# Local and pooled attention with a mixture of experts on one core: the first steps in another order, and the first slot's chain divided over the last two units

## The chip, the cores and the metric

The kernel runs on one core of a Trainium2 chip. The metric is the time of one launch on the device in microseconds. TensorE (PE in the rows) does the matrix products and transposes, VectorE (DVE) reductions and elementwise work, ScalarE (ACT) activations and copies, GpSimd (POOL) elementwise work and indirect transfers, and SyncE (SP) issues the plain transfers. The engines run beside one another; each takes its own instructions in the order of the program.

## The reference

The first half is two attentions over q, k and v of 8 batches, 8 heads, 576 positions and 64 features. One sees only the positions closer than 4; the other works on means over groups of 4 positions, and its result is repeated 4 times. Their sum, with the heads side by side, is x, 4608 rows of 512. The second half sends each row to one of 8 experts and weights the answer:

```python
mask = np.abs(pos[:, None] - pos[None, :]) < factor
attn_out = out_up + out_local
logits = xn @ en.T / tau              # xn, en: rows over their norms
expert_idx = np.argmax(logits, axis=1)
h = np.maximum(x[mask] @ w1[e], 0.0)
out[mask] = gate_w[mask, None] * (h @ w2[e])
```

## The kernel before

**Attention.** A unit is one batch and one pair of heads; there are 32, numbered 0 to 31. The function attention (lines 182 to 331 of the file before) is a loop over i from -2 to 32, and each step i holds one stage of three or four units: the transposes of q and k for unit i+2 (qk_T, L378, whose four results ACT copies out of PSUM at L379), the scores of unit i+1 (scores L407 and L412, scores_d L434 for the pooled half), and the weights and values of unit i (weights_T L485, weights_dT L496, values_d L505, values L521); rows (L536, L539) brings unit i-1 back to rows and forms logits. ACT and DVE do the softmax between them: the copies aT (L488) and adT (L498), the exponentials (L425, L454), the sums, their inverses, and the products an (L472) and ad (L477). od (L511) is the pooled result and xr (L543) the rows. The order of the Python statements is the order of each engine's queue; nothing else reorders it.

**Banks.** Every product goes to one of 7 PSUM banks of one pool (bank), handed out in rotation: a product that takes the bank of seven allocations ago waits until that one has been read. In a usual step the third bank of weights_T is that of the first of qk_T's four, so PE waits there for ACT's first copy of L379.

**Guests in the steps.** Between the steps the loop yields its place (i, k), and other generators run. first_weights (L904 to L970) brings expert 0's w1 and w2 in, in four pieces each: it loads a piece, squares it on ACT (L859) for a scale, adds up over partitions with one product (total, L868), works the power of two out on DVE (scales, L876 and L878, which ends in the tile wscl), and splits each piece into two f16 halves: the high one on ACT (split_h, L882), the low one on DVE one step later (split_l, L887). The three tuples FREE, LIGHT and HEAVY name the steps, modulo 4, in which the next piece may come. early_slots (L711 to L744) takes its turns at the places listed in EARLY. A slot is a block of 128 rows of one expert; the first three are filled from batches 0 to 5 while the attention still runs: limits, indices (ids_of, L702), a gather of rows on POOL (L1126), and then for slot 0 the chain x_size (a sum of squares on ACT, L1144, and a power of two on DVE, L79 to L81) and x_split (x's high half on ACT, L1153, its low half on DVE, L1156, and a transposing transfer, L1158). The first product of the experts (mm1_half, L1205 to L1207) needs that transfer.

**The start.** load brings q and k of 4 heads (two units), load_v and load_w bring v in two layouts. Constants are made on POOL and DVE meanwhile. warm_up (L337) is a number of products of 128x512 zeros whose results nobody reads.

Of the kernel before, what the change touches and what calls it, by code (L numbers as in the profile page):

```python
# [43 lines left out]
FIRST = 3  # L44
EARLY = ((28, 0), (28, 1), (29, 0), (30, 3), (31, 0), (31, 1))
MASKED = -1.0e30
# [5 lines left out]
class Kern:  # L52
# [55 lines left out]
    def constants_rows(self):  # L108
# [14 lines left out]
        nc.vector.memset(self.enT, 0.0)  # L123
        yield
# [56 lines left out]
    def attention(self, ctx):  # L181
# [28 lines left out]
        def load_w(j):  # L210
            if j < n // 2:
                self.load_w(j // 2, j % 2, self.vw[j % 2])

        load(0)
        nc.vector.memset(self.w1h[:, 0, :512], 0.0)
# [17 lines left out]
        next(crows)  # L233
        load_v(0)
        load(1)
        load_w(0)
        tail, mid = [], []
        for i in range(-2, n + 1):
            a, c, d, e = i + 2, i + 1, i, i - 1
            if a < n:  # L240
                st[a] = {"u": a, "j": a % 2, "vw": self.vw[a // 2 % 2], **half[a // 2]}
                self.qk_T(st[a])
            if a == n:
                self.warm_up(2)
# [4 lines left out]
            if a < n:  # L249
                self.pooled(st[a])  # L250
                for u in range(a if a > 1 else 0, a + 1 if a else 0):
                    self.pooled_v(st[u])
                if a % 2:
                    load_v(a // 2 + 1)
            if i in (0, 2):
                next(clists)
            if 0 <= d < n:
                self.weights_T(st[d])
            if 0 <= c < n:
                self.scores_d(st[c])  # L260
                self.exps(st[c])
                self.peaks_d(st[c])
# [25 lines left out]
            if c == n - 1:  # L288
                self.sums_l(st[c])
                self.inverses(st[c])  # L290
                self.normalise_l(st[c])
                self.normalise_d(st[c])
                yield i, 3
            if 0 <= c < n - 1:
# [18 lines left out]
            if 0 <= c < n - 1:  # L313
                self.normalise_d(st[c])
            if i == n - 1:
                tail.pop(0)()
            if i == -1:
                next(crows)
                nc.vector.memset(self.lg, 0.5)
                nc.vector.memset(self.oh, 0.0)  # L320
# [391 lines left out]
    def early_slots(self):  # L712
# [22 lines left out]
        yield  # L735
        self.x_size(0)
        self.norms(0)
        self.x_split(0)
        yield
# [160 lines left out]
    def first_weights(self):  # L900
# [53 lines left out]
        square(1, 2, 3)  # L954
        yield FREE
        self.total(slice(1, 2))
        self.scales(slice(1, 2))
        yield HEAVY
        split(1, 0)
# [5 lines left out]
        split(1, 3)  # L965
        self.out_scale()
        for i in range(2):
# [168 lines left out]

    def x_size(self, q):
        nc, s = self.nc, self.sl[q]
        xg = s["xg"]
        v = nc.vector  # L1140
        ss = s["ss"] = self.mx.tile([SLOT, 1], F32, name="ss", bufs=4)
        sc = s["sc"] = self.mx.tile([SLOT, 1], F32, name="sc", bufs=4)
        lg = s["lg"] = self.mx.tile([SLOT, E], F32, name="lg", bufs=4)
        nc.scalar.activation(out=self.jk[:, :DM], in_=xg[:, :DM], func=AF.Square, accum_out=ss)  # L1144
        v.tensor_copy(out=lg, in_=xg[:, DM:])
        self.pow2(self.mx, ss, sc)

    def x_split(self, q, other=None):
        nc, s = self.nc, self.sl[q]
        xs = s.pop("xg")[:, :DM]  # L1150
        v, sc = nc.vector, s["sc"]
        x2 = self.mx.tile([SLOT, 2, DM], F16, name="x2")
        nc.scalar.activation(out=x2[:, 0], in_=xs, func=AF.Copy, scale=sc)  # L1153
        if other is not None:
            self.logits(other)
        v.scalar_tensor_tensor(out=x2[:, 1], in0=xs, scalar=sc, in1=x2[:, 0], op0=ALU.mult, op1=ALU.subtract)  # L1156
        xT = s["xT"] = self.mx.tile([128, 2, self.KC, SLOT], F16, name="xT2", bufs=3)
        nc.sync.dma_start_transpose(out=xT.rearrange("p t c s -> p (t c) s"), in_=x2.rearrange("p a f -> p (a f)"))  # L1158
# [87 lines left out]
    def run(self):  # L1246
# [9 lines left out]
        with ExitStack() as actx:  # L1256
# [3 lines left out]
            for at in steps:  # L1260
# [4 lines left out]
                i, end = at  # L1265
                if end and i >= 1 and i % NHP in heavy:
                    heavy = next(w0, ())
# [107 lines left out]
```

## Time and profile before

| | us |
|---|---|
| median of 3 runs | 730.81 (727.73 to 730.84) |
| profiled execution | 730.06 |
| its span, first to last instruction | 728.1 |
| TensorE busy in the span | 698.2 (96%) |
| VectorE, ScalarE, GpSimd busy | 464.4, 466.7, 403.7 |

The attention fills the span up to about 272 us; from there on the experts' products follow one another. In the timeline rows below, the first column is the start in us from the span's start and the second the time from the first start to the last end of the merged instructions; the bracket gives how long the engine had nothing to do before it and what ended that.

### The profile page before, as it was taken

Reading aid. Unit: us, or ns where it says so; the run is one execution under the profiler, and the core shown is the slowest. Engines: PE = TensorE matmul, PEld = TensorE weight load, DVE = VectorE, ACT = ScalarE, POOL = GpSimd, SP = SyncE. Lnnn points to the kernel's source line nnn. Section 1 sums busy time; section 2 is a strip of 40 time slices with the busy share of each in tenths; the row PEclk is TensorE's granted clock in tenths of the full one; section 3 lists DMA queues with packets and bytes.
Section 4 is the critical chain, followed back from the end, with each engine's and each line's share of the span. In section 5 each row is a group of like instructions: output and inputs, shape, how many; then the busy total and the mean of one; then the engine's idle time right before and its main releaser. Section 6 shows DMA issues by size and latency. Waiting matters only on the chain. (4 is left out here: it accounts for less than half of the span.)

```text
span 728.1 us, 27458 instructions
## 1 busy us (share of the span) xinstructions
PE 698.2 (96%) x10501; PEld 527.0 (72%) x10501; DVE 464.4 (64%) x1395; ACT 466.7 (64%) x1095; POOL 403.7 (55%) x800
## 2 busy tenths in 40 slices
PE   8998999999999989999999999999999999999993
PEld 5787787787878667677767767766776776777671
DVE  6777788797898958757446466564754375456420
ACT  4787877888877654556746658576673367357520
POOL 8554646765776916547543554556465535535421
PEclk9999999999999879999999999999999999999997
DMA  8999887999968357344826566386673346348300
GB/s 192 196 239 255 177 225 161 257 246 196 236 154 226 86 185 212 89 101 165 184 78 200 167 185 187 103 242 113 181 171 87 90 165 177 90 126 214 60 31 20
DMA packets 191238, 117.82 MB, mean 162 GB/s; under 512 B 162898, under 2 KB 162898, under 8 KB 191072
## 3 DMA queue, kind: packets, MB, share of 16 engines
q1 hardware_dynamic: 183264, 94.61, 53.1%
q0 software_dynamic: 6560, 19.03, 8.4%
q10 hardware_dynamic: 1248, 2.11, 1.0%
q8 instruction: 85, 1.39, 0.8%
q14 instruction: 81, 0.66, 0.3%
HBM read 213.12 MB, written 20.33 MB: 321 GB/s over the span
## 5 line engine op out<-in xcount | busy, mean ns | idle before, releaser
L1207 PE MATMUL bank<-xT,w1l 128*128 128x128 f16 x1312 | 223.3, 219 | 2.9 <-DVE w1l L887 1.4
L1206 PE MATMUL bank<-xT,w1h 128*128 128x128 f16 x1312 | 223.5, 219 | 0.4 <-issue 0.3
L1205 PE MATMUL bank<-xT,w1h 128*128 128x128 f16 x1312 | 223.6, 219 | 0.0
L1205 PEld LDWEIGHTS <-w1h 128*128 128x128 f16 x1312 | 128.6, 98 | 7.0 <-issue 2.4
L1207 PEld LDWEIGHTS <-w1l 128*128 128x128 f16 x1312 | 128.6, 98 | 5.0 <-DVE w1l L887 2.6
L1206 PEld LDWEIGHTS <-w1h 128*128 128x128 f16 x1312 | 128.6, 98 | 4.1 <-issue 0.5
L1230 PE MATMUL bank<-w2h,hT 128*128 128x512 f16 x328 | 124.3, 379 | 0.0
L1229 PE MATMUL bank<-w2l,hT 128*128 128x512 f16 x328 | 124.2, 379 | 0.0
L1228 PE MATMUL bank<-w2h,hT 128*128 128x512 f16 x328 | 124.2, 379 | 0.0
L1242 POOL DMA_INDIRECT out_dram<-o,ids x40 | 51.0, 1274 | 111.8 <-ACTq L1042 74.3
L1217 DVE SCALAR_TENSOR_TENSOR hT<-bank,hT 128x512 f16<-128x512 f32 x82 | 54.9, 686 | 44.3 <-ACT hT L1216 19.7
L1216 ACT ACTIVATE hT<-bank 128x512 f16<-128x512 f32 x82 | 46.6, 587 | 51.0 <-PE bank L868 33.1
L392 POOL TENSOR_TENSOR pool_kq<-kq 128x288 f32<-128x288 f32 x62 | 40.2, 670 | 56.4 <-ACT kq L379 54.7
L1156 DVE SCALAR_TENSOR_TENSOR x<-xg,sc,x 128x512 f16<-128x512 f32 x41 | 30.8, 751 | 60.1 <-ACT x L1153 52.9
L859 ACT ACTIVATE junk<-st 128x1024 bf16<-128x1024 f32 (+1 forms) x30 | 67.5, 2248 | 2.1 <-POOL at L618 1.6
L1126 POOL DMA_INDIRECT xg<-xd,ids x41 | 44.4, 1083 | 38.7 <-POOLq L1048 17.2
L401 POOL TENSOR_TENSOR pool_v<-ld_v 72x256 f32<-72x256 f32 x64 | 54.6, 873 | 18.7 <-DMA ld_v<-in_v_dram 17.1
L1230 PEld LDWEIGHTS <-hT 128*128 128x128 f16 x328 | 32.0, 98 | 38.7
L1228 PEld LDWEIGHTS <-hT 128*128 128x128 f16 x328 | 32.0, 98 | 33.8
L1229 PEld LDWEIGHTS <-hT 128*128 128x128 f16 x328 | 32.0, 98 | 33.8
L1174 ACT ACTIVATE lg<-lg,lmx 128x8 f32<-128x8 f32 x41 | 12.3, 300 | 66.8 <-DVE lmx L1172 65.6
L488 ACT ACTIVATE aT<-bank 70x384 f32<-70x384 f32 x96 | 40.1, 486 | 20.9 <-PE bank L485 20.8
(238 smaller groups left out, 1519.3 us busy)
## 6 DMA issues: line engine op xcount, KB each, us to landing
st<-in_moe_w_dram SPq DMA_DIRECT2D x148, 1024.0 KB
ld_k<-in_k_dram SPq DMA_DIRECT2D x64, 144.0 KB
ld_q<-in_q_dram SPq DMA_DIRECT2D x64, 144.0 KB
ld_v<-in_v_dram SPq DMA_DIRECT2D x16, 576.0 KB
vw<-in_v_dram SPq DMA_DIRECT2D x16, 576.0 KB
xd<-xr SPq DMA_DIRECT2D x8, 1040.0 KB
st<-in_moe_w_dram SPq DMA_DIRECT2D x12, 512.0 KB
st<-in_moe_w_dram ACTq DMA_DIRECT2D x4, 512.0 KB
```

Source lines behind the costliest of these rows:

```text
L401: g.tensor_tensor(out=t6[:, h], in0=vr[:, :, 0:2 * D], in1=vr[:, :, 2 * D:], op=ALU.add)
L859: self.nc.scalar.activation(out=junk, in_=src, func=AF.Square, accum_out=acc)
L1126: nc.gpsimd.indirect_dma_start(out=xg, out_offset=None, in_=self.xd[:n], in_offset=bass.IndirectOffsetOnAxis(ap=self.ids[:, q:q + 1], axis=0),
L1205: nc.tensor.matmul(out=o, lhsT=self.w1h[:, k, f], rhs=xT[:, 0, k], start=(k == 0), stop=False)
L1206: nc.tensor.matmul(out=o, lhsT=self.w1h[:, k, f], rhs=xT[:, 1, k], start=False, stop=False)
L1207: nc.tensor.matmul(out=o, lhsT=self.w1l[:, k, f], rhs=xT[:, 0, k], start=False, stop=(k == self.KC - 1))
L1216: nc.scalar.activation(out=h[:, 0], in_=ps, func=AF.Relu)
L1217: nc.vector.scalar_tensor_tensor(out=h[:, 1], in0=ps, scalar=0.0, in1=h[:, 0], op0=ALU.max, op1=ALU.subtract)
L1228: nc.tensor.matmul(out=ps, lhsT=hh, rhs=self.w2h[:, j, :], start=(j == 0), stop=False)
L1229: nc.tensor.matmul(out=ps, lhsT=hh, rhs=self.w2l[:, j, :], start=False, stop=False)
L1230: nc.tensor.matmul(out=ps, lhsT=hl, rhs=self.w2h[:, j, :], start=False, stop=(j == self.FC - 1))
L1242: nc.gpsimd.indirect_dma_start(out=self.out, out_offset=bass.IndirectOffsetOnAxis(ap=self.ids[:, q:q + 1], axis=0), in_=o, in_offset=None, ...
```

## The change

**First steps.** Step -1 and step 0 now do the scores of unit i+1 before anything else. Step -2 transposes unit 0 as before, step -1 transposes unit 1 after the scores of unit 0, and step 0 puts the transposes of unit 2, with their pooling, behind everything else of the step. The products of zeros fall from 8, 3 and 7 to 8 and 2, and the two at the end of the attention go too. The scaling of the expert embedding (en, one instruction of 8x512) and the memset of enT go from DVE to POOL, and their transposes to the end of step 0. load_w(0) is issued ahead of load(1).

```diff
-            if a < n:
-                st[a] = {"u": a, "j": a % 2, "vw": self.vw[a // 2 % 2], **half[a // 2]}
-                self.qk_T(st[a])
-            if a == n:
-                self.warm_up(2)
-            if 0 <= c < n:
+            if i in (-1, 0):
                 self.scores(st[c])
-                if not c:
-                    self.warm_up(3)
+            if i:
+                transposed(a)
+            if 1 <= c < n and i:
+                self.scores(st[c])
+            if a < n and i:
+                pooled(a)
...
-                    self.warm_up(7)
+                    self.warm_up(2)
...
+            if not i:
+                transposed(a)
+                pooled(a)
+                next(crows)
...
-        nc.vector.tensor_scalar(out=en, in0=en, scalar1=inv, scalar2=None, op0=ALU.mult)
+        nc.gpsimd.tensor_scalar(out=en, in0=en, scalar1=inv, scalar2=None, op0=ALU.mult)
...
+        load_w(0)
         load(1)
-        load_w(0)
```

transposed and pooled are new local functions that hold the lines taken out (qk_T of a unit; pooling of k, q and v and the next load of v).

In PE's queue, right behind the eight products of zeros at the start (kq_107 is unit 0's transposed q and k, kq_111 unit 1's, identb and mask open the scores), the kernel before has:

```order
L378 MATMUL bank<-ident,ld_k 128x96 x6
L378 MATMUL bank<-ident,ld_q 128x96 x6
L378 MATMUL bank<-ident,ld_k 128x96 x6
L378 MATMUL bank<-ident,ld_q 128x96 x6
L407 LDWEIGHTS identb
L407 MATMUL bank<-mask,identb 128x342
L412 MATMUL bank<-kq_107 32x38 x36
L337 LDWEIGHTS w1h
L337 MATMUL bank<-w1h 128x512
```

The changed kernel has there:

```order
L391 MATMUL bank<-ident,ld_k 128x96 x6
L391 MATMUL bank<-ident,ld_q 128x96 x6
L420 LDWEIGHTS identb
L420 MATMUL bank<-mask,identb 128x342
L425 MATMUL bank<-kq_107 32x38 x36
L391 MATMUL bank<-ident,ld_k 128x96 x6
L391 MATMUL bank<-ident,ld_q 128x96 x6
L447 MATMUL bank<-kqd 72x144 x4
L420 LDWEIGHTS identb
L420 MATMUL bank<-mask,identb 128x342
L425 MATMUL bank<-kq_111 32x38 x36
L498 MATMUL bank<-ident,an_109 70x128 x9
```

Unit 1's transposes stand behind unit 0's scores, no product of zeros follows them, and unit 1's scores come before unit 0's weights without unit 2's transposes between.

**First expert's weights.** The scale of w1 and the split of its first piece now come in one turn, in step 8; the same holds for w2 in step 19. The splits of w1 end in step 15 instead of 16, those of w2 are in steps 19, 20, 23 and 24 instead of 23, 24, 27 and 28, and the loads of the second expert's w1 that follow come in steps 25 and 26 instead of 29 and 30.

```diff
         square(0, 2, 3)
-        yield FREE
+        yield HEAVY
         self.total(slice(0, 1))
         self.scales(slice(0, 1))
         self.keep_scale()
-        yield HEAVY
         split(0, 0)
```

In ACT's queue, from the end of step 8 into step 9, the kernel before has (kq_111 are the four copies of unit 11's transposes):

```order
L511 ACTIVATE od<-bank 128x144
L543 ACTIVATE xr<-bank 128x4x128
L379 ACTIVATE kq_111<-bank 128x288 x4
L488 ACTIVATE aT<-bank 70x384 x3
L425 ACTIVATE a<-a 128x342
```

and the changed kernel:

```order
L524 ACTIVATE od<-bank 128x144
L556 ACTIVATE xr<-bank 128x4x128
L900 ACTIVATE w1h<-st_740,wscl 128x2x512
L392 ACTIVATE kq_111<-bank 128x288 x4
L501 ACTIVATE aT<-bank 70x384 x3
L438 ACTIVATE a<-a 128x342
```

The split stands between xr and the copies of kq, and it reads wscl.

**First slot.** EARLY has nine places instead of six. The limits and the indices' parts come one turn earlier, in steps 27 and 28. Slot 0's chain is cut in four: the sum of squares at the head of ACT's work in step 30, the power of two and the norms after the scores, the high half after the weights' transposes, and the low half and the transfer at the end of the step.

```diff
-EARLY = ((28, 0), (28, 1), (29, 0), (30, 3), (31, 0), (31, 1))
+EARLY = ((27, 0), (28, 0), (29, 0), (30, 4), (30, 5), (30, 0), (30, 3), (31, 0), (31, 1))
...
-        self.x_size(0)
+        self.x_square(0)
+        yield
+        self.x_scale(0)
         self.norms(0)
-        self.x_split(0)
+        yield
+        self.x_high(0)
+        yield
+        self.x_low(0)
```

The place (30, 3) itself moves from before unit 31's sums_l to the end of the step. In ACT's queue, step 30, the kernel before has (junk,ss is slot 0's sum of squares, x_6006 its high half):

```order
L543 ACTIVATE xr<-bank 128x4x128
L488 ACTIVATE aT<-bank 70x384 x3
L425 ACTIVATE a<-a 128x342
L454 ACTIVATE ad,sums_114<-bank,md 72x144 x4
L498 ACTIVATE adT<-bank 72x288 x2
L1144 ACTIVATE junk,ss<-xg 128x512
L1153 ACTIVATE x_6006<-xg,sc 128x512
L511 ACTIVATE od<-bank 128x144
```

and the changed kernel:

```order
L556 ACTIVATE xr<-bank 128x4x128
L1161 ACTIVATE junk,ss<-xg 128x512
L501 ACTIVATE aT<-bank 70x384 x3
L438 ACTIVATE a<-a 128x342
L467 ACTIVATE ad,sums_114<-bank,md 72x144 x4
L511 ACTIVATE adT<-bank 72x288 x2
L1179 ACTIVATE x_5975<-xg,sc 128x512
L524 ACTIVATE od<-bank 128x144
```

The sum of squares, which reads the gathered rows xg, stands ahead of aT.

## Rows read from the trace of the kernel before

**Rows 1.** The page's first line: busy time of each engine, its share of the span, and its instructions.

```profile
PE 698.2 (96%) x10501; PEld 527.0 (72%) x10501; DVE 464.4 (64%) x1395; ACT 466.7 (64%) x1095; POOL 403.7 (55%) x800
```

**Rows 2.** The view of waits, PE alone, whole span: who waited, for whom, us in total, times, longest.

```profile
PE bank L496 <- ACT od L511: 2.0, 1, 2.0
PE bank L378 <- ACT od L511: 1.9, 2, 1.5
```

**Rows 3.** The timeline of PE, first 26 us.

```profile
5.83 1.19 PE L378 MATMUL bank<-ident,ld_q 96*128 96x96 f32 x6
...
9.89 1.37 PE L412 MATMUL bank<-kq 64*32 64x38 f32 x72
11.19 1.46 PE L337 MATMUL bank<-w1h 128*128 128x512 f16 x3
12.58 1.24 PE L434 MATMUL bank<-kqd 64*72 64x144 f32 x8
...
14.23 0.71 PE L378 MATMUL bank<-ident,ld_k 96*128 96x96 f32 x6
...
17.60 1.15 PE L485 MATMUL bank<-ident,an 128*70 128x128 f32 x9 [1.23 <-DVE an L472]
...
19.93 1.68 PE L337 MATMUL bank<-w1h 128*128 128x512 f16 x7
...
25.30 1.18 PE L485 MATMUL bank<-ident,an 128*70 128x128 f32 x9
```

**Rows 4.** The timelines of DVE and ACT, first 21 us.

```profile
7.45 1.49 DVE L121 TENSOR_SCALAR en<-en,eninv 8x512 f32<-8x512 f32 x1
...
16.42 1.03 DVE L472 TENSOR_TENSOR an<-a,inv 64x342 f32<-64x342 f32 x2
...
20.05 0.69 ACT L498 ACTIVATE adT<-bank 72x288 f32<-72x288 f32 x2
```

**Rows 5.** The timelines of PE, ACT and DVE where step 8 ends and step 9 begins.

```profile
86.88 0.30 PE L407 MATMUL bank<-mask,identb 128*128 128x342 bf16 x1 [0.59 <-DVE xT L523]
...
87.90 1.18 PE L485 MATMUL bank<-ident,an 128*70 128x128 f32 x9
...
84.91 0.59 ACT L543 ACTIVATE xr<-bank 128x512 f32<-128x512 f32 x1
85.65 1.32 ACT L379 ACTIVATE kq<-bank 128x288 f32<-128x288 f32 x4
...
88.18 0.14 DVE L878 TENSOR_SCALAR wscl<-wk 128x1 int32<-128x1 int32 x1
```

**Rows 6.** The same timelines where step 18, with two squares at its end, goes over into step 19.

```profile
165.85 0.52 PE L485 MATMUL bank<-ident,an 128*70 128x128 f32 x3 [0.16 <-ACT kq L379]
...
165.41 1.29 ACT L379 ACTIVATE kq<-bank 128x288 f32<-128x288 f32 x4
```

**Rows 7.** The instructions of line 882 up to 260 us: duration in ns, least, median and most, and first and last start.

```profile
L882 ACT ACTIVATE w1h<-st,wscl x4: 1149/1149/1151, 108.5 to 147.9; 128x1024 f16<-128x1024 f32 x4
```

**Rows 8.** The timeline of PE, steps 29 to 31 and the first product of the experts.

```profile
242.75 0.47 PE L378 MATMUL bank<-ident,ld_q 96*128 96x96 f32 x3 [0.38 <-ACT od L511]
...
247.76 0.90 PE L702 MATMUL bank<-parts,at 128*128 128x6 bf16 x30 [0.94 <-DVE a L424]
...
253.47 1.03 PE L337 MATMUL bank<-w1h 128*128 128x512 f16 x2
...
260.82 0.76 PE L505 MATMUL bank<-adT,vd 72*64 72x144 f32 x8 [0.71 <-ACT adT L498]
...
265.78 0.98 PE L496 MATMUL bank<-ident,ad 72*72 72x72 f32 x8 [2.05 <-ACT od L511]
...
271.78 0.27 PE L1205 MATMUL bank<-xT,w1h 128*128 128x128 f16 x1
```

**Rows 9.** The timelines of ACT, DVE and POOL there: weights' copies, slot 0's sum of squares, od; the first gather; and on SP's queue the transposing transfer of the second slot.

```profile
257.20 1.24 ACT L488 ACTIVATE aT<-bank 70x384 f32<-70x384 f32 x3 [3.33 <-PE bank L485]
...
260.94 0.64 ACT L1144 ACTIVATE junk<-xg 128x512 bf16<-128x512 f32 x1
...
265.44 0.29 ACT L511 ACTIVATE od<-bank 128x144 f32<-128x144 f32 x1 [1.36 <-DVE ls L548]
...
251.31 1.27 POOL L1126 DMA_INDIRECT xg<-xd,ids  x1 [0.30 <-DVE lmx L588]
...
274.27 1.24 SPq L1158 DMA_TRANSPOSE xT<-x  x1
```

**Rows 10.** The view by stretches of 1 us: length, busy us of PE, PEld, DVE, ACT and POOL with their counts, the clock granted to TensorE (1.00 is 2.4 GHz, 0.50 is 1.2 GHz), the share of the DMA engines, GB/s.

```profile
219.00:220.00 1.00, 0.98 (x40) 0.59 (x42) 0.96 (x3) 1.00 (x4) 0.33 (x1) 0.50 1.05 301
...
250.00:251.00 1.00, 1.00 (x14) 0.61 (x8) 0.93 (x6) 0.32 (x2) 0.92 (x2) 0.50 0.00 0
...
267.00:268.00 1.00, 1.00 (x8) 0.57 (x10) 0.00 (x0) 1.00 (x4) 0.00 (x0) 0.50 1.02 188
...
277.00:278.00 1.00, 1.00 (x21) 1.00 (x19) 0.86 (x6) 0.81 (x2) 0.00 (x0) 1.00 0.00 0
```

**Rows 11.** POOL's sums over v beside no split and beside a split on DVE, and, from the view of line 1126 between 240 and 420 us (18 gathers), the time from issue to landing.

```profile
230.31 1.42 POOL L401 TENSOR_TENSOR pool_v<-ld_v 72x256 f32<-72x256 f32 x2
238.46 2.94 POOL L401 TENSOR_TENSOR pool_v<-ld_v 72x256 f32<-72x256 f32 x2
...
DMA to landing us min/median/max: 5.0/7.6/10.3
```

More of the change, by code (lines that the diff above doesn't have):

```diff
@@ L120, in constants_rows @@
         nc.vector.reciprocal(out=inv, in_=self.norm(nc.vector, c, ss, 1e-6))
-        nc.vector.tensor_scalar(out=en, in0=en, scalar1=inv, scalar2=None, op0=ALU.mult)
+        nc.gpsimd.tensor_scalar(out=en, in0=en, scalar1=inv, scalar2=None, op0=ALU.mult)
         self.enT = c.tile([128, NHP, 32], F32, name="enT")
-        nc.vector.memset(self.enT, 0.0)
+        nc.gpsimd.memset(self.enT, 0.0)
         yield
@@ L212, in load_w, with transposed, pooled @@
                 self.load_w(j // 2, j % 2, self.vw[j % 2])
+        def transposed(a):
+            if a < n:
+                st[a] = {"u": a, "j": a % 2, "vw": self.vw[a // 2 % 2], **half[a // 2]}
+                self.qk_T(st[a])
+        def pooled(a):
+            self.pooled(st[a])
+            for u in range(a if a > 1 else 0, a + 1 if a else 0):
+                self.pooled_v(st[u])
+            if a % 2:
+                load_v(a // 2 + 1)
         load(0)
@@ L239, in attention @@
             a, c, d, e = i + 2, i + 1, i, i - 1
-            if a < n:
-                st[a] = {"u": a, "j": a % 2, "vw": self.vw[a // 2 % 2], **half[a // 2]}
-                self.qk_T(st[a])
-            if a == n:
-                self.warm_up(2)
-            if 0 <= c < n:
-                self.scores(st[c])
-                if not c:
-                    self.warm_up(3)
[L249 to L254, printed above, removed]
+            if i in (-1, 0):
+                self.scores(st[c])
+            if i:
[4 more added lines that the diff above has]
+                pooled(a)
             if i in (0, 2):
                 next(clists)
+            if c == n - 1:
+                yield i, 4
             if 0 <= d < n:
@@ L261, in attention @@
                 self.exps(st[c])
+                if c == n - 1:
+                    yield i, 5
                 self.peaks_d(st[c])
@@ L314, in attention @@
                 self.normalise_d(st[c])
+            if c == n - 1:
+                yield i, 3
             if i == n - 1:
                 tail.pop(0)()
+            if not i:
+                transposed(a)
+                pooled(a)
+                next(crows)
             if i == -1:
-                next(crows)
                 nc.vector.memset(self.lg, 0.5)
@@ L954, in first_weights @@
         square(1, 2, 3)
-        yield FREE
+        yield HEAVY
         self.total(slice(1, 2))
         self.scales(slice(1, 2))
-        yield HEAVY
+        self.out_scale()
         split(1, 0)
@@ L1137, in x_size, with x_square, x_scale, x_high @@
     def x_size(self, q):
+        self.x_square(q)
+        self.x_scale(q)
+    def x_square(self, q):
         nc, s = self.nc, self.sl[q]
         xg = s["xg"]
-        v = nc.vector
         ss = s["ss"] = self.mx.tile([SLOT, 1], F32, name="ss", bufs=4)
+        nc.scalar.activation(out=self.jk[:, :DM], in_=xg[:, :DM], func=AF.Square, accum_out=ss)
+    def x_scale(self, q):
+        s = self.sl[q]
         sc = s["sc"] = self.mx.tile([SLOT, 1], F32, name="sc", bufs=4)
         lg = s["lg"] = self.mx.tile([SLOT, E], F32, name="lg", bufs=4)
-        nc.scalar.activation(out=self.jk[:, :DM], in_=xg[:, :DM], func=AF.Square, accum_out=ss)
-        v.tensor_copy(out=lg, in_=xg[:, DM:])
-        self.pow2(self.mx, ss, sc)
+        self.nc.vector.tensor_copy(out=lg, in_=s["xg"][:, DM:])
+        self.pow2(self.mx, s["ss"], sc)
     def x_split(self, q, other=None):
[L1149 to L1153, printed above, removed]
+        self.x_high(q)
         if other is not None:
             self.logits(other)
-        v.scalar_tensor_tensor(out=x2[:, 1], in0=xs, scalar=sc, in1=x2[:, 0], op0=ALU.mult, op1=ALU.subtract)
+        self.x_low(q)
+    def x_high(self, q):
+        s = self.sl[q]
+        x2 = s["x2"] = self.mx.tile([SLOT, 2, DM], F16, name="x2")
+        self.nc.scalar.activation(out=x2[:, 0], in_=s["xg"][:, :DM], func=AF.Copy, scale=s["sc"])
+    def x_low(self, q):
+        nc, s = self.nc, self.sl[q]
+        xs, x2 = s.pop("xg")[:, :DM], s.pop("x2")
+        nc.vector.scalar_tensor_tensor(out=x2[:, 1], in0=xs, scalar=s["sc"], in1=x2[:, 0], op0=ALU.mult,
+                                       op1=ALU.subtract)
         xT = s["xT"] = self.mx.tile([128, 2, self.KC, SLOT], F16, name="xT2", bufs=3)
@@ L1265, in run @@
                 i, end = at
-                if end and i >= 1 and i % NHP in heavy:
+                if end == 1 and i >= 1 and i % NHP in heavy:
                     heavy = next(w0, ())
```

2 lines of the change are left out of this document (removed).

## The prediction

> **What bounds the kernel now.** The page's first line comes first: PE is busy 698.2 us of a span of 728.1, 96% [rows 1]. No other engine is above 64%, so time is to be won only where PE stands idle or runs at the low clock. The view of waits for PE says where that is [rows 2]: the longest waits are single ones, at two banks that od frees. The timelines of PE place them: one wait of 1.23 before the first weights [rows 3], short ones in the middle [rows 5, 6], and a group from 242 us to the first expert product at 271.78 [rows 8]. Behind 271.78 the experts' products follow one another, and nothing of the change lies there; so the end moves as that start moves. The view by stretches adds the second cost: the clock is at 0.50 (1.2 GHz) at 250 and again at 267, in each case just after PE idled 0.94 and 2.05 [rows 8, 10]. What a fall costs I read at the start: three products of zeros took 1.46, seven took 1.68 [rows 3], 487 against 240 ns each. A low stretch holding work worth 1.7 at 2.4 GHz thus costs 1.7 more.
>
> All sums are made against the profiled execution, 730.06, which is its span and 2.0 around it; the median of the runs is 0.75 above. By 0.5% (3.65 us) a measurement of this kernel can tell a change from none.
>
> **Start: −0.6.** Unit 0's transposes end at 5.83 + 1.19 = 7.02 [rows 3]. Its scores need only their copies (some 0.45, an estimate: a quarter and more of 1.32 [rows 5]) and begin near 7.5; before they stood behind unit 1's transposes and ended at 9.89 + 1.37 = 11.26. They wait for nothing on DVE: en, which kept it until 8.94 [rows 4], is now on POOL, where nothing of PE needs it before the end of step 0, though POOL's pooling for step -1 is queued behind it; at twice its 1.49 it is still over before 11.5. Unit 1's transposes (about 2.1 at the low clock) follow, the three zeros (1.46) are gone, and scores_d starts near 10.95 where it started at 12.58. The chain from there to weights_T(0), by way of an (16.42 + 1.03 [rows 4]), took 17.60 − 12.58 = 5.02 and is unchanged: 15.95. From the first weights to the second is 25.30 − 17.60 = 7.70 before. Five zeros leave (5 × 0.24 = 1.2), but values_d behind them waits for adT, over at 20.74 [rows 4], so I count 0.75. Into this stretch come unit 2's transposes (1.05, the first 0.71 in [rows 3]), en's (0.3) and a wait of some 0.4 for banks: 8.7. Weights_T(1) begins near 24.65, 0.65 early. Bounds: −1.7 if the banks cost nothing and the zeros free their whole 1.2; +2.2 if, with 2.2 of idle ahead of the first weights instead of 1.23 and eight fewer zeros, the clock rises one stretch later (1.7 more, and a wait).
>
> **Middle: +3.6.** In step 8 ACT is free at 84.91 + 0.59 = 85.50 and begins the four copies of kq at once [rows 5]. The changed order puts the first split of w1h ahead of them. It waits for wscl, ready at 88.18 + 0.14 = 88.32 [rows 5], and takes 1.15 [rows 7]: the copies begin at 89.5 instead of 85.65. Behind the waiting split on ACT stand those copies, aT and the exponentials. PE waits at the third bank of weights_T, which is that of the first copy: it comes there 0.8 (two thirds of 1.18) after 87.90, at 88.7, and the bank is free at about 90.0. That is 1.3; later in the step values_d waits for a late adT, say 0.5; together 1.8. The low bound is the place where two squares already stand in front of the copies: these begin at 165.41, and PE waited 0.16 [rows 6]. The high bound is 1.8 and one fall of the clock, 3.5. ACT itself idles 88.32 − 85.50 = 2.8 there. Of the two ends I take the worked one, as in rows 6 no wait for DVE stood before the copies. The same comes at step 19 for w2: another 1.8. The squares that move from step 19 to 16 cancel. The sum is +3.6, bounds +0.4 and +7.0.
>
> **Tail: −3.9.** The limits move to step 27 and lengthen it on DVE: the 0.38 at 242.75 may become 0.9. But the splits of w2 are out of steps 27 and 28 by then, and with them ACT's 1.15 ahead of the copies; the stall of 0.94 at 247.76 goes [rows 8], the clock has no cause to fall at 250, and the two zeros at 253.47 (1.03, of which some 0.8 counts) are gone. Weights_T(30) can then start near 252.5; it started at 256.6, just ahead of aT's copies at 257.20 [rows 9].
>
> In its place comes a new wait. ACT's work in step 30 now opens with the sum of squares, which reads gather 0; aT, the exponentials and adT are queued behind it, and PE's values_d waits for adT. The gather was issued at 251.31 [rows 9]. POOL's sums over v take 1.42 where no split runs on DVE and 2.94 beside one [rows 11]; 251.31 − 1.52 − 0.94 − 0.38 gives 248.5 for the issue. Of 18 gathers the fastest landed 5.0 after issue, the median 7.6, the slowest 10.3 [rows 11]. I take 5.0 to 6.0, as this one is the first in its queue: it lands at 253.5 to 254.5. With 0.85 for the sum of squares (0.64 and its read-out [rows 9]) aT starts at 254.4 to 255.4 and values_d(30), which before came 260.82 − 257.20 = 3.62 behind aT, at 258.0 to 259.0; take 258.7, 2.1 early. PE idles some 2.4 before it, where it idled 0.71.
>
> Behind that the chain is shorter. The scale, high and low half no longer stand between unit 31's products and ls, for which od waited 1.36 [rows 9]: od comes at about 261.4 and not 265.44. The 2.05 before the last weights shrinks to about 1.3. From there to the first expert product was 271.78 − 265.78 = 6.0 at mostly 1.2 GHz; at 2.4 GHz it is 4.0 and a wait of some 0.3 for adT: 266.1. The transposing transfer of slot 0 must have landed too: its low half now stands behind DVE's last two additions for od, some 1.8 behind od's start by an estimate, and ends near 263.2, and the second slot's transfer, issued at 274.27, had no packets left at 277 [rows 9, 10]: 2.7 later is 265.9, and some completion time behind it. So it becomes late next, by a hair, and I put the start at 266.6: −5.2. Then the clock: the new idle of 2.4 is like the 2.05 that was followed by 0.50, and I charge 1.3 (1.7 at three chances in four). Sum −3.9. Bounds: −6.9 if the gather lands early enough that ACT never waits; +1 if it needs 7.6 or more.
>
> The Trainium skill speaks to this wait: "DMA: Bandwidth & Descriptors", section "Anatomy of one DMA — SWDGE (gpsimd) path", gives an indirect transfer of POOL's a fixed 2.0 us and its bytes over 436 GB/s. For 266 KB that is 2.6 us, an estimate from that page: the gather would land at 251.1, ACT would not wait, and the tail would be 1.7 better, the whole 727.5. The eighteen gathers of this trace took at least 5.0, so the measurement decides, and the sum keeps it.
>
> **Sum.** 730.06 − 0.6 + 3.6 − 3.9 = 729.2; with the larger part of the doubtful clock in it I say 729.3.
>
> **Rivals.** *A, the middle costs nothing.* The banks' rotation lets PE run ahead far enough that a late copy costs 0.16 to 0.4, as at the squares [rows 6], twice; and the clock holds in the tail: −0.6 + 0.8 − 5.2 gives 725.1. For it: PE's margin was already enough there once. Against: the squares waited for nothing, the split waits 2.8 for wscl. Chance 0.27. *B, the gather is late.* If it lands at the median, 248.5 + 7.6 = 256.1, ACT's queue is held until 256.95 and values_d(30) starts at 260.6, as before; PE has idled 4.6, the clock is low for what follows, and the tail brings nothing: 730.06 − 0.6 + 3.6 + 0 is 733.1, and with 10.3, 735.8. It decides from a landing about 7 us after issue. For it: over half the gathers were that late, and a store of x runs on the transfer queues at the same time. Against: they were mostly one of three in a row or beside weights. Chance 0.20; I price it at 734. *C, the landing of the page named above*, 727.5, inside what can be told from no change: 0.05. *D, the start doesn't do what it says*: the scores wait for a bank or for their copies, the clock rises late, and its +2.2 adds to the forecast: 732.1, still within. Chance 0.02. My forecast has 0.46, with a range of its own from 726.5 to 733.
>
> **How the numbers follow.** A is faster in nine cases of ten and the forecast's lower edge adds little: faster 0.28. B is slower in eight cases of ten, and the forecast with the middle near its high bound adds 0.05: slower 0.21. The rest, 0.51, cannot be told from no change. The range that leaves out a tenth on each side goes from 724.5 (A with a little of the start's better bound) to 734.8 (B between its two landings).
>
> **What would show it.** In the trace of the changed kernel: scores of unit 0 at 7.5, the first weights at 16.0 and the second at 24.6; ACT's split waiting some 2.8 for wscl in steps 8 and 19 and PE waiting for the copies of kq right after, 1.3 each; sums over v at 1.4 in steps 27 and 28, the first gather issued near 248.5, ACT's sum of squares idle before it until xg lands, od at 261 to 262, the first expert product at 266 to 267. The forecast is wrong if PE doesn't wait after the two splits (then A), if the gather takes over 7 us (then B), or if the clock shows 0.50 in the middle, where each fall adds 1.7.

## The result and the profile after

The changed kernel is slower: 736.09 us in the median of 20 runs, against 730.83 for the kernel before; the ratio is 1.0069, with a 95% interval from 1.0045 to 1.0094, that is +3.3 to +6.9 us. Forecast were 729.3 and a range from 724.5 to 734.8. The profiled execution took 734.89, its span 733.1. The profiles of start_alone and split_apart_again, named below, are of launches over 1.5% longer than the fastest of their kernel, and no stage is read from them.

The page's first line, which answers to [rows 1]:

```profile
PE 697.5 (95%) x10491; PEld 526.3 (72%) x10491; DVE 462.5 (63%) x1393; ACT 466.9 (64%) x1095; POOL 405.3 (55%) x802
```

PE was busy 0.7 us less than before, with ten products of zeros fewer; time at the low clock counts as busy. Its idle time in the span grew by 5.7 us. The view of waits for PE, which answers to [rows 2] (who waited, for whom, us in total, times, longest):

```profile
PE bank L425 <- issue: 3.5, 6, 0.9
PE bank L498 <- DVE an L485: 2.7, 1, 2.7
PE bank L498 <- ACT kq L392: 2.4, 3, 1.1
PE bank L518 <- ACT adT L511: 1.9, 2, 1.2
PE bank L391 <- ACT od L524: 1.8, 2, 1.5
PE bank L534 <- issue: 1.5, 1, 1.5
...
PE bank L549 <- issue: 1.1, 1, 1.1
PE bank L391 <- issue: 1.0, 1, 1.0
```

and of the same view for the kernel before:

```profile
PE bank L496 <- issue: 1.8, 1, 1.8
...
PE bank L485 <- DVE an L472: 1.2, 1, 1.2
PE bank L485 <- issue: 1.2, 1, 1.2
...
PE bank L485 <- ACT kq L379: 0.3, 2, 0.2
```

The wait for an, ahead of the first weights, has grown by 1.5, the wait for kq's copies from 0.3 to 2.4. Stalls for which the rows name nothing ("issue") stand in both kernels; they add up to 7.1 us in that view, 4.5 before. The timeline of PE, first 44 us (start, us, what, idle time before it), which answers to [rows 3]:

```profile
6.70 0.30 PE L420 MATMUL bank<-mask,identb 128*128 128x342 bf16 x1
...
13.41 2.10 PE L498 MATMUL bank<-ident,an 128*70 128x128 f32 x9 [2.74 <-DVE an L485]
...
23.91 1.18 PE L498 MATMUL bank<-ident,an 128*70 128x128 f32 x9
...
35.90 0.76 PE L518 MATMUL bank<-adT,vd 72*64 72x144 f32 x8 [1.24 <-ACT adT L511]
...
37.86 1.22 PE L391 MATMUL bank<-ident,ld_k 96*128 96x96 f32 x6
```

The first weights come 4.19 us earlier, but take 2.10 instead of 1.15: the clock is at 1.2 GHz behind the idle 2.74. The second come 1.39 earlier. At 37.86 six transposes take 1.22 instead of some 0.7: the clock has fallen again, behind a wait of 1.24 that was 0.53 before. The view by stretches (columns as in [rows 10]) has it at 0.50 there:

```profile
38.00:39.00 1.00, 1.00 (x7) 1.00 (x8) 0.95 (x3) 0.53 (x2) 0.21 (x1) 0.50 0.91 200
```

Where step 8 goes over into step 9, the timelines of ACT, DVE and PE read as follows; they answer to [rows 5]:

```profile
86.55 0.59 ACT L556 ACTIVATE xr<-bank 128x512 f32<-128x512 f32 x1
89.99 1.15 ACT L900 ACTIVATE w1h<-st,wscl 128x1024 f16<-128x1024 f32 x1 [2.85 <-DVE wscl L896]
91.05 1.29 ACT L392 ACTIVATE kq<-bank 128x288 f32<-128x288 f32 x4
...
89.81 0.15 DVE L896 TENSOR_SCALAR wscl<-wk 128x1 int32<-128x1 int32 x1
...
91.49 0.52 PE L498 MATMUL bank<-ident,an 128*70 128x128 f32 x3 [1.11 <-ACT kq L392]
```

ACT idles 2.85 before the split, and PE 1.11 at the third bank behind it; 86 us later the same comes with 2.61 and 1.10.

The timelines of SP, POOL, PE and ACT in steps 27 to 31, which answer to [rows 8, 9, 11]:

```profile
235.14 3.22 SPq L1007 DMA_DIRECT2D st<-in_moe_w_dram  x4
238.46 0.35 SPq L367 DMA_DIRECT2D ld_v<-in_v_dram  x1
239.17 8.87 SPq L377 DMA_DIRECT2D vw<-in_v_dram  x3
...
248.38 1.41 POOL L414 TENSOR_TENSOR pool_v<-ld_v 72x256 f32<-72x256 f32 x2 [4.19 <-DMA ld_v<-in_v_dram]
...
257.94 1.27 POOL L1142 DMA_INDIRECT xg<-xd,ids  x1 [0.30 <-DVE lmx L601]
...
248.43 0.39 PE L534 MATMUL bank<-aT,vw 70*64 70x64 f32 x5 [1.50 <-issue]
...
262.29 0.53 PE L425 MATMUL bank<-kq 64*32 64x38 f32 x29 [0.46 <-issue]
...
268.46 0.76 PE L518 MATMUL bank<-adT,vd 72*64 72x144 f32 x8 [0.70 <-ACT adT L511]
...
276.12 0.23 PE L1234 MATMUL bank<-xT,w1h 128*128 128x128 f16 x1 [0.76 <-DMA xT<-x]
...
263.52 0.63 ACT L1161 ACTIVATE junk<-xg 128x512 bf16<-128x512 f32 x1 [3.02 <-DMA xg<-xd,ids]
```

Here is what the prediction did not price. Four loads of the second expert's w1, 2 MB by the page's sizes, now stand on SP's queue right ahead of the last loads of v, those of units 30 and 31. ld_v lands 9.9 us behind its issue (248.38 − 238.46), POOL's sums over v idle 4.19 for it, and at the same moment PE stalls 1.50 in the products that read vw. The clock is at 0.50 behind that:

```profile
250.00:251.00 1.00, 1.00 (x6) 0.58 (x5) 0.00 (x0) 0.86 (x3) 1.00 (x2) 0.50 0.10 19
264.00:265.00 1.00, 1.00 (x7) 0.55 (x6) 0.46 (x3) 1.00 (x5) 0.50 (x3) 0.50 0.39 150
```

(the view by stretches, columns as in [rows 10]). The first expert product starts at 276.12 instead of 271.78, 4.34 late. From there to the end both kernels need about the same, 456.98 and 456.32.

Not all of that is made in step 28. The weights' transposes of unit 28 start there, first in the kernel before, then in the changed one:

```profile
236.25 1.18 PE L485 MATMUL bank<-ident,an 128*70 128x128 f32 x9
```

```profile
241.83 1.18 PE L498 MATMUL bank<-ident,an 128*70 128x128 f32 x9
```

The changed kernel is 5.58 late there already. The next table takes the two profiles apart at the starts of the weights' transposes, in us, with the terms of the prediction beside them.

| from the weights of unit | before | changed | difference | forecast |
|---|---|---|---|---|
| (start of the span) to 1 | 25.30 | 23.91 | −1.39 | −0.65 |
| 1 to 4 | 22.39 | 26.06 | +3.67 | none |
| 4 to 8 | 31.69 | 31.06 | −0.63 | none |
| 8 to 11 (first waiting split) | 23.36 | 26.11 | +2.75 | +1.8 |
| 11 to 19 | 62.09 | 60.71 | −1.38 | none |
| 19 to 22 (second waiting split) | 24.05 | 24.52 | +0.47 | +1.8 |
| 22 to 28 | 47.36 | 49.46 | +2.10 | none |
| 28 to the first expert product | 35.53 | 34.29 | −1.24 | −3.9 |

From unit 28's weights to unit 29's, where the stall of 1.50 lies, the changed kernel takes 10.47, the kernel before 8.05, and the nine kernels below with slot 0's change and the old turns of the weights 8.30 to 8.32. The whole last stage is shorter than before all the same, as the three units behind it take 23.8 together instead of 27.5.

### The profile page after: what moved, and what is told of

It reads as the page before. It is cut to its first block, busy times and chain, and to the rows that moved or that the text cites. A ratio compares the mean times of both kernels' runs of the same rounds, so it can differ in the third digit from the quotient of the medians.

```text
span 733.1 us, 27440 instructions
## 1 busy us (share of the span) xinstructions
PE 697.5 (95%) x10491; PEld 526.3 (72%) x10491; DVE 462.5 (63%) x1393; ACT 466.9 (64%) x1095; POOL 405.3 (55%) x802
## 3 DMA queue, kind: packets, MB, share of 16 engines
q8 instruction: 85, 1.39, 0.8%
## 5 line engine op out<-in xcount | busy, mean ns | idle before, releaser
L414 POOL TENSOR_TENSOR pool_v<-ld_v 72x256 f32<-72x256 f32 x64 | 50.1, 801 | 34.4 <-DMA ld_v<-in_v_dram 28.7
L70 POOL TENSOR_SCALAR nw_t<-nw_y,nw_a 128x1 f32<-128x1 f32 x123 | 46.7, 380 | 12.4
```

The lines of the kernel that those rows point to most:

```text
L70: g.tensor_scalar(out=t, in0=y, scalar1=y, scalar2=a, op0=ALU.mult, op1=ALU.mult)
L414: g.tensor_tensor(out=t6[:, h], in0=vr[:, :, 0:2 * D], in1=vr[:, :, 2 * D:], op=ALU.add)
```

## The experiments

Each was timed in five rounds beside the kernel before on the same chip, so the intervals are some 0.3% to either side, and a profile of each is read by stages: the starts of the weights' transposes of unit 1, 4, 8 and so on, up to the first expert product. The middle stretches between (units 4 to 8 and 11 to 19) differ by up to 6 us among profiles, by falls of the clock and stalls of PE that come and go; the stages named below repeat.

**The three parts alone.** *start_alone* has the new first steps on the kernel before, *weights_alone* the new turns of the weights, *slot_alone* slot 0's change; *no_weights* is the changed kernel without the new turns. Each is a part of the diff shown ahead of the prediction; the products of zeros taken out at the attention's end go with the first steps. Of the turns the core is:

```diff
-        yield FREE
+        yield HEAVY
         self.total(slice(0, 1))
         self.scales(slice(0, 1))
         self.keep_scale()
-        yield HEAVY
         split(0, 0)
```

> The kernel before with the new first steps alone; the weights' turns and slot 0's chain are as before. By the sum of the prediction the second weights begin near 24.6 and the whole is 0.6 us faster. By the theory from the changed kernel's trace (the casts of the constants on DVE in step 2 now run beside POOL's pooling, PE waits over 1 us for adT near 35.9 and the clock falls for what follows) the second weights begin near 23.9, but the fourth near 41.5 instead of 40.5, and the whole is 1 to 2.5 us slower. If the first steps are harmless and the fall of the clock there was a chance, the fourth weights begin near 39 and it is 1.4 us faster.

> The kernel before with the weights' turns alone. Theory of the splits (ACT's split waits for wscl ahead of the copies of kq): PE waits about 1.1 at the third bank of the weights in steps 9 and 20, +2.2 to +3.6 us in all, and nothing more. Theory of the loads (the loads of the second expert's w1, now in steps 25 and 26 instead of 29 and 30, crowd v's load of step 28): besides that POOL's sums over v idle about 4 us for ld_v in step 28, PE stalls over 1 us there and the clock is at 0.50 near 249 to 252, another 2 to 4 us, so +4.5 to +7 in all. If neither holds, within 1 us of before.

> The kernel before with the divided chain of slot 0 and the earlier limits alone. By the prediction's tail (the last waits shrink, the chain is shorter) 3.9 us faster less what the old splits of w2 in steps 27 and 28 cost, so 2 to 4 us faster. By the theory of the gather (the sum of squares at ACT's head waits for xg, 5 to 6 us after its issue, and PE waits for adT behind it) ACT idles about 3 us before the sum of squares, the last step is no shorter, and the whole is within 1.5 us of before.

> The changed kernel with the weights' turns of before. If the weights' turns carry most of the loss, the median comes back to within 1.5 us of the kernel before, PE has no wait of 1.1 for ACT's copies of kq in steps 9 and 20, and v's load of step 28 lands in time. If the start and the tail carry it, it stays 3 us or more slower. By the prediction's terms without the middle it would be 4.5 us faster.

Measured: start_alone 1.0010 (0.9977 to 1.0043), weights_alone 1.0090 (1.0058 to 1.0122), slot_alone 0.9993 (0.9960 to 1.0025), no_weights 1.0009 (0.9980 to 1.0037). The weights' turns carry the loss; of the two other parts neither a gain nor a loss is clear of noise. The prediction's terms would have made slot_alone 2 to 4 us faster and no_weights 4.5; neither came. weights_alone shows the two waits of 1.11, and in step 28 this, on POOL and PE:

```profile
248.19 1.41 POOL L401 TENSOR_TENSOR pool_v<-ld_v 72x256 f32<-72x256 f32 x2 [5.18 <-DMA ld_v<-in_v_dram]
...
247.56 1.06 PE L521 MATMUL bank<-aT,vw 70*64 70x64 f32 x15 [1.65 <-issue]
```

**The two halves of the turns.** *weights_late_loads* keeps the loads in steps 29 and 30; *weights_split_apart* puts each first split one step behind its scale and leaves the loads early; *both_apart* does both.

```diff
+        for _ in range(4):
+            yield FREE
         for i in range(2):
             yield FREE
             for j in range(2):
                 self.stage(0, slice(1, 2), 2 * i + j, 4)
```

```diff
         self.scales(slice(0, 1))
         self.keep_scale()
+        yield FREE
         split(0, 0)
...
         self.out_scale()
+        yield FREE
         split(1, 0)
-        yield HEAVY
+        yield FREE
         split(1, 1)
```

> The kernel before with the weights' turns of the change, but the loads of the second expert's w1 stay in steps 29 and 30. Theory of the loads (4 MB of weights ahead of v's last loads on SP's queue cost a stall of 1.65 and a stretch at 1.2 GHz in step 28, and more transfers before): about half or more of the 6.6 us of weights_alone comes back, so +2 to +3.5 us over before, and the two waits of 1.11 in steps 9 and 20 stay. Rival, the splits carry all: +5.5 to +7 us. In the trace, ld_v of step 28 lands within 4 us of its issue by either theory; only by the first does PE lose its stall of over 1 us near 247.

> The turns of the change, but each first split one step behind its scale, so that ACT doesn't wait for wscl; the loads of the second expert's w1 stay in steps 25 and 26 as in the change. Theory of the splits: the two waits of 1.11 are gone and +3.5 us or less over before remains. Theory of the loads: the stall of over 1 us in step 28 stays and with it the larger part, +4 to +6 us. The two theories together: weights_late_loads and this one add up to about the 6.6 us of weights_alone.

> The kernel before with the turns of the change, but both suspected costs taken out: each first split one step behind its scale, and the loads of the second expert's w1 in steps 29 and 30. If these two are all that makes the weights' turns dear, the median is within 2 us of the kernel before, steps 8 to 11 and 19 to 22 take what they took before (14.8 and 24.1 us), and PE has no stall of over 1 us in step 28. If moving the other splits and w2's squares costs too, it stays 2.5 us or more above.

Measured: 1.0028 (0.9989 to 1.0067), 1.0029 (0.9992 to 1.0066) and 0.9972 (0.9934 to 1.0011). (The page's sizes make the loads 2 MB, not the 4 that the expectation says, and the 14.8 us of the last expectation are those of units 9 to 11.) As the whole and its halves came from different chips, they were timed again side by side:

> weights_alone once more, beside its two halves on one chip. Against the kernel before +4 to +8 us, with the two waits of 1.11 in steps 9 and 20 and a stall of over 1 us in step 28.

> weights_late_loads beside weights_alone on one chip. If the loads carry over half of the loss it is 3.5 us or more below weights_again; if the splits carry over half, less than 3 us below it.

> weights_split_apart beside weights_alone on one chip. If the loads carry over half of the loss it is less than 3 us below weights_again; if the splits carry over half, 3.5 us or more.

Measured: 1.0112 (1.0071 to 1.0152), 1.0068 (1.0033 to 1.0102), 1.0072 (1.0030 to 1.0115). Taking away either half brings 0.6% the first time and 0.4% the second, some 3 to 4.5 us, and taking away both brings the kernel back to before. Each of these differences is uncertain by about 0.5%, so how the loss divides between the halves is known only roughly. That each half costs something is shown by the last two kernels, which have one half each and lie above the kernel before, beside both_apart, which has neither. Neither theory of one cause stands.

The profiles place both. Units 8 to 11 take 23.4 us in the kernel before and in all without a waiting split (23.6 in the four with the split apart), and 25.7 to 26.1 in the five with it: +2.3 to +2.7 around the wait in step 9. Units 19 to 22 take 24.05 before and 25.1 to 26.2 in the four kernels with the weights' turns alone and a waiting split, but 24.52 in the changed kernel. From unit 28's weights to the first expert product the kernels with the old chain of slot 0 take 37.5 in the mean of three profiles with early loads (36.6 to 37.9) and 34.7 in the mean of four with late ones (33.9 to 35.5): +2.7. In weights_late_loads POOL's last sums come without that wait, and with the split apart it stays; first the one, then the other:

```profile
239.87 1.41 POOL L401 TENSOR_TENSOR pool_v<-ld_v 72x256 f32<-72x256 f32 x2
246.92 1.43 POOL L401 TENSOR_TENSOR pool_v<-ld_v 72x256 f32<-72x256 f32 x2
```

```profile
242.70 1.76 POOL L401 TENSOR_TENSOR pool_v<-ld_v 72x256 f32<-72x256 f32 x2 [4.78 <-DMA ld_v<-in_v_dram]
```

This 2.7 belongs to the kernel before with the turns alone. In the changed kernel the stage took 34.29, against 35.3 to 35.7 in the five kernels with its slot chain and the old turns, and no run takes the early loads alone out of it.

The loads reach PE by more than one way. In weights_alone it was a stall put down to "issue". In weights_split_apart it was POOL's at, late behind those sums (0.40 twice, near 248). weights_again, the same program as weights_alone, has no long stall in step 28 either, against its expectation; PE waited 0.40 for POOL's at.

What PE waits for when a stall is put down to "issue" no view names, but the transfers in the trace make one cause likely. The page of each kernel lists a queue of 85 packets, 16 KB each (here the changed kernel's line: packets, MB, share):

```profile
q8 instruction: 85, 1.39, 0.8%
```

In the 18 profiles used here, 58 such stalls of 0.6 us or more lie ahead of 280 us, and all 58 ended 1.2 to 1.65 us after one of these packets had ended. A moment taken at random between 60 and 250 us lies so in 8 of 100 cases. The stall of 1.50 in the changed kernel ended at 248.43, the packet at 246.97; the longest stall of the kernel before ended at 66.39, the packet at 64.95. So PE most likely waited for its own instructions. That the moved loads delayed them in step 28 is argued from the place, not shown.

**The tail.** *square_behind* is no_weights with the sum of squares back behind adT and the rest of slot 0's chain at the end of the step; *gather_clear* is no_weights with the second expert's loads another step later; *slot_behind* is the kernel before with slot 0's change and the sum of squares behind adT.

```diff
-EARLY = ((27, 0), (28, 0), (29, 0), (30, 4), (30, 5), (30, 0), (30, 3), (31, 0), (31, 1))
+EARLY = ((27, 0), (28, 0), (29, 0), (30, 0), (30, 3), (31, 0), (31, 1))
...
         self.norms(0)
-        yield
-        self.x_high(0)
-        yield
-        self.x_low(0)
+        self.x_split(0)
```

```diff
+        yield FREE
         for i in range(2):
             yield FREE
             for j in range(2):
```

> no_weights with slot 0's sum of squares back behind adT (and its scale, high and low half at the end of step 30). Theory of the gather (7.2 us from issue to landing, the sum of squares at ACT's head holds aT and PE idles 2.05 behind it): that wait goes, PE reaches the expert products 1.5 to 3 us earlier, and the median is 1 to 3 us below no_weights. Rival, VectorE sets the last steps (PE waited 2.17 for an of unit 30 before): the time moves into od and the first product's transfer and the median stays within 1 us of no_weights.

> no_weights with the loads of the second expert's w1 one step later (30 and 31 instead of 29 and 30), so that 2 MB of weights are not on the way when slot 0 is gathered. If those loads are what makes the gather land 7.2 us after its issue, it lands in 5 to 6 us, ACT's idle time before the sum of squares falls from 4.66 to about 3, and PE's wait of 2.05 behind it to under 1; the median falls by 0 to 2 us. If the store of x is what delays it, it stays at 7 us and nothing changes.

> The kernel before with slot 0's change alone, the sum of squares back behind adT. If the gather's wait is what ate the tail's gain, it is 1 to 3 us faster than the kernel before (slot_alone was equal to it). If VectorE and POOL set the last steps, as PE's wait for an of unit 30 says, it stays within 1 us of it, and the first product of the experts comes 42 to 43.5 us behind the 27th unit's weights, as in all kernels so far.

Measured: 0.9975 (0.9936 to 1.0014), 0.9993 (0.9958 to 1.0029), 0.9959 (0.9927 to 0.9992); only the last is clear of the kernel before. In no_weights the gather was issued at 251.12, not earlier than before, and ACT and PE read:

```profile
258.34 0.63 ACT L1163 ACTIVATE junk<-xg 128x512 bf16<-128x512 f32 x1 [4.66 <-DMA xg<-xd,ids]
```

```profile
254.36 1.26 PE L498 MATMUL bank<-ident,an 128*70 128x128 f32 x9 [2.17 <-DVE an L485]
...
259.49 0.70 PE L509 MATMUL bank<-ident,ad 72*72 72x72 f32 x4 [2.05 <-ACT aT L501]
```

7.2 us lie between issue and use; in gather_clear, with no weights on the way, again 7.2 (258.00 to 265.24), so the loads are not what delays it. In slot_behind the sum of squares finds its rows there, and PE's wait is elsewhere:

```profile
258.79 0.64 ACT L1152 ACTIVATE junk<-xg 128x512 bf16<-128x512 f32 x1
```

```profile
253.68 1.15 PE L490 MATMUL bank<-ident,an 128*70 128x128 f32 x9 [1.85 <-DVE an L477]
...
265.21 1.15 PE L510 MATMUL bank<-adT,vd 72*64 72x144 f32 x8 [1.64 <-ACT adT L503]
```

Timed side by side the two slot kernels say:

> slot_alone once more, beside slot_behind on one chip. Against the kernel before within 1.5 us; ACT idles 4 to 5 us before slot 0's sum of squares, PE over 2 us for aT behind it.

> slot_behind beside slot_alone on one chip. If the sum of squares at ACT's head is what ate the gain of slot 0's change, 1.5 to 4 us below slot_again and 1.5 us or more below the kernel before; if its first result was chance, within 1 us of slot_again.

Measured: 0.9985 (0.9954 to 1.0017) and 1.0002 (0.9970 to 1.0034). The second theory's price did not repeat in the median. In the profiles it does: from unit 28's weights to the first expert product the five kernels with the sum of squares at ACT's head and the old turns of the weights take 35.3 to 35.7, the five with it behind adT 32.2 to 34.4. So 2.3 us of wait are shown in that stage; that they shorten the launch is not.

**Repairs together.** *start_warm* is no_weights with five products of zeros ahead of the first weights; *together* adds the casts of step 2 in two turns and the sum of squares behind adT; *mended* is the changed kernel with the three repairs to weights and slot (their diffs are those above).

```diff
+            if not d:
+                self.warm_up(5)
             if 0 <= d < n:
                 self.weights_T(st[d])
```

```diff
             v.tensor_copy(out=d, in_=i)
+            if i is pi:
+                yield
...
-            if i in (0, 2):
+            if i in (0, 2, 3):
                 next(clists)
```

> no_weights with five products of zeros in PE's idle time of 2.74 us ahead of the first weights. If that idle time is what brings the clock to 0.50 between 12 and 18 us (to 28 in one run), the stretch goes, the second weights begin near 22.5 instead of 23.4 to 27.0, and the median falls by 1 to 2.5 us. If the clock is low there whatever PE does, or if the zeros hold up the first weights, nothing changes.

> The version that the runs point to: weights' turns of before, the new first steps with the five zeros, the constants' casts of step 2 divided over steps 2 and 3 (1.9 to 2.3 us of DVE work in one step made PE wait 0.3 to 1.3 for adT there), and slot 0's sum of squares behind adT. If the three mechanisms are right, 2 to 5 us faster than the kernel before, and PE waits less than 0.3 for adT in step 2. If the clock's falls come anyway, within 1.5 us of it.

> The whole change with three repairs: each first split one step behind its scale, the loads of the second expert's w1 in steps 29 and 30, and slot 0's sum of squares behind adT. If these three places are where the change lost, it is 1.5 to 4 us faster than the kernel before. If the new first steps or the earlier limits lose as well, it is within 1 us of it.

Measured: 1.0004 (0.9979 to 1.0029), 0.9960 (0.9939 to 0.9982), 0.9987 (0.9949 to 1.0024). The zeros do what was expected of them on the clock, and the idle time behind them is 1.55, but the second weights begin at 24.62 and not near 22.5: PE waits 0.63 for POOL's sums and 0.65 and 0.35 at the transposes between. The rows of start_warm beside that of the changed kernel (columns as in [rows 10]):

```profile
14.00:15.00 1.00, 1.00 (x14) 0.76 (x11) 0.96 (x5) 1.00 (x3) 0.92 (x2) 1.00 0.92 175
```

```profile
14.00:15.00 1.00, 1.00 (x7) 0.86 (x5) 0.96 (x5) 0.58 (x2) 1.00 (x2) 0.50 0.51 105
```

Unit 4's weights then start at 47.50 and 47.14 (start_warm and together); with the new first steps without the zeros they start at 46.2 to 50.0, with the old ones at 47.0 to 49.3. The median of start_warm shows nothing of it. together's interval lies below the kernel before: 728.29, some 3 us faster. The only other such result, slot_behind's first, did not repeat, and together was timed once. mended, expected 1.5 to 4 us faster, shows neither gain nor loss, so the three repairs take the loss away and bring no gain. together's wait for adT in step 2 is gone, but a wait of 1.07 for DVE stands in step 3.

## Why the prediction was wrong

**Start, −0.6: no gain measured, the mechanism right.** Scores began at 6.70 (7.5 said), the first weights at 13.41 (15.95), the second at 23.91 (24.65): both estimates were too late. The price that was put into the bound, a clock that stays low behind more idle time, came: 2.74 of idle instead of 2.2, and 0.50 behind it. The casts of step 2 are older than the change (0.53 before); in the changed kernel they took PE 1.24 and the clock. By unit 4 the changed kernel was 2.3 late (49.97 against 47.68). start_alone: +0.1%, and its interval holds zero as well as the −0.6.

**Middle, +3.6: confirmed.** ACT idled 2.85 and 2.61 (2.8 said), PE waited 1.11 and 1.10 (1.3), the stages around them grew by 2.3 to 2.7 and, the second, by 1.1 to 2.2 in four kernels and 0.47 in the changed one (1.8 each). Timed, the splits carry some 3 to 4.5 us. Rival A, that the banks hide ACT's wait, is out.

**The step that failed first: what the moved turns carry with them.** The prediction said that "the splits of w2 are out of steps 27 and 28 by then", booked that as a gain, and stopped there. The loads behind them in the same generator move as well, from steps 29 and 30, where no loads of q, k and v are left, to SP's queue ahead of the last v. It priced them at nothing; on the kernel before they cost some 3 to 4.5 us timed, 2.7 by the profiles' stage. In the sum of the prediction, 729.2 + 3.5 would have been 732.7, still not to be told from no change; only without the tail's 3.9 as well is it 736.6, beside the 736.09 measured. So two terms failed, this one and the tail.

**Tail, −3.9: with the old turns of the weights nothing, in the changed kernel −1.24 by its one profile.** Counted from the start of unit 28's weights, the gather's issue was forecast at 12.25 (248.5 − 236.25) instead of 15.06. In the changed kernel POOL's sums are short (1.41, 1.40) as said, but POOL waited 4.19 for ld_v, and the issue came at 16.11 (257.94 − 241.83): by this profile the step that was missed also took most of what the tail was to bring. Behind the issue the forecast held there, 18.2 us to the first expert product, where 18.1 were said and 20.5 lay before. Part of that is luck: PE waited 0.70 for adT and not 2.4, but lost 1.9 to short stalls in unit 31's scores.

With the old turns three numbers of the chain fell. In no_weights POOL's sums stay long (2.72, 2.86), as the old splits are there, and the issue came at 251.12, 14.92 behind unit 28's weights. Its landing, 5.0 to 6.0 behind, was 5.6 in the changed kernel and 7.2 to 7.5 in the kernels with the old turns, so rival B's mechanism holds wherever the weights' turns are the old ones: aT was late, PE waited 2.05 for it in no_weights, and slot_alone came out even, as B said of the tail. And weights_T(30), said to be free to start at 252.5, waited 1.85 to 2.17 for DVE's an in slot_alone, slot_behind, no_weights and together: DVE sets step 29 there, and a PE that is early only waits. The transposing transfer did become "late next, by a hair": PE waited 0.76 for it in the changed kernel. Rival C, a landing after 2.6 us, is out too: this gather took 5.6 to 7.5 in all profiles in which ACT waited for it.

Rival C came from the Trainium skill, "DMA: Bandwidth & Descriptors", section "Anatomy of one DMA — SWDGE (gpsimd) path"; the traces do not agree with the estimate of 2.6 from it, as this gather took 5.6 to 7.5. The prediction prices a gather for which ACT never waits in two ways that don't agree, −6.9 in the tail's bounds and 1.7 better than −3.9 in rival C.

**Chances.** Slower had 0.21, of it 0.16 for B and 0.05 for the middle near its high bound; the range ended at B's price, 734.8, since a second cause for slower was not among the rivals.

What stays open: what delays the packets ahead of the long stalls without a name, and what the short ones of some 0.5 in unit 31's scores are; why the gather landed 1.6 us sooner in the changed kernel than elsewhere; whether the 2.3 us at the tail show in the time, as two timings disagree; and what slot 0's chain and the early loads are each worth in the changed kernel itself.

## What to carry to other kernels

When a turn of a generator moves, everything behind it moves: list the transfers it issues at the end, and look whose loads they now stand ahead of on the same queue. A step put at the head of an in-order engine must have its input there, or the rest of the step waits with it; its old place, behind work that others need, was a cover and not a delay. And time won ahead of a stage is worth nothing if another engine sets that stage: read its own waits once the earlier stall is thought away.

## What the runs showed that was not expected

Stages that a change leaves alone gain or lose several us by falls of the clock and stalls that land elsewhere from profile to profile: units 4 to 8 took 30.4 to 35.8 us among these profiles, and units 11 to 19 60.5 to 66.6. A wait of 1.24 was followed by 1.2 GHz in the changed kernel, one of 1.11 in step 9 was not. An earlier start of 4.2 us at the first weights was gone by the fourth unit.
